# Packed attention and a channel mixer: the first phase's loads in blocks of 128 partitions, and w1 on ScalarE's queue

## The chip, the core and the metric

The kernel runs on one core of one Trainium2 chip: TensorE (PE) for products, VectorE (DVE), ScalarE (ACT) and GpSimd (POOL) for elementwise work, SyncE (SP) to issue transfers, and 16 DMA engines between DRAM and SBUF. SBUF has 128 partitions. Times are device microseconds of one execution. The kernel before took a median of 899.99 us in 3 runs (896.8 to 904.1).

## The reference

Eight batches, eight heads, 576 tokens, 64 numbers per head. 32 packed queries `p` per head attend over all tokens; the 576 queries `q` then attend over the 32 packed results. The heads are joined to 512 columns, and a mixer follows.

```python
def sm_attn(qq, kk, vv):
    s = scale * np.matmul(qq, kk.transpose(0, 1, 3, 2))
    a = np.exp(s - np.max(s, axis=-1, keepdims=True))
    a = a / (np.sum(a, axis=-1, keepdims=True) + 1e-09)
    return np.matmul(a, vv)
p_packed = sm_attn(p, k, v)                 # 8 x 8 x 32 x 64
out = sm_attn(q, p_packed, p_packed)        # 8 x 8 x 576 x 64
# x: 8 x 576 x 512, the heads joined
xt = x.transpose(0, 2, 1)
h = xt @ U @ V                              # over tokens, rank 32
u = x + h.transpose(0, 2, 1)
ch = np.maximum(u @ w_ch1, 0.0) @ w_ch2     # 512 -> 2048 -> 512
return u + ch
```

q, k, v and p are float32. U, V, w_ch1 and w_ch2 come as float64; the kernel reads them as pairs of 32-bit words (`I32`, 8 bytes a number) and makes float32 of them on the chip.

## The kernel before, in words

**Two parts.** The first part works on 16 units, one for each batch and group of four heads (`UN`). A unit loads k (`a_load`, `kx`) and v (`a_load_v`, `vt`), turns k with TensorE (`a_turn`, L205), makes the scores of the packed queries (`a_scores`), their exponentials (`a_softmax`), turns those back (`a_turn_back`), multiplies with v (`a_pack`, L451) and turns the result (`a_heads`). The packed result of each batch goes to DRAM (`ppTd`) and comes back when it is wanted (`ppT`). In the loop of this part (L486) the units are staggered: in iteration i unit i gets its scores, unit i+1 is turned, unit i+2's k and unit i+1's v are asked for. k and v have three buffers each.

Beside the units the first part brings in w1 (`w_ch1`), in 16 pieces of 128 rows by 512 numbers (512 KB of float64 words each): `load_w1` brings the bits, `convert_w1` makes float32 of them with one ScalarE (L75) and four VectorE instructions (L76 to L79). One piece is converted in each iteration (`some_w1`), and the piece two further on is asked for. The bits have two buffers, `bits`, which w2's pieces and the output share later. U and V are loaded in iteration 2 (`load_uv`). From iteration 5 the steps of the attention of batch 0 (`attention(0, res)`, whose first step loads q) run two at a time; in iteration 16 batch 1's q is asked for.

The second part (from L524) goes over 8 batches and 16 blocks of the 2048 hidden columns: `gemm1` (`h_ps`, L84 to L86) and `gemm2` (`o`), each as three float32r products, with the attention of the next batch worked in between as steps, q of the batch after that asked for at block 13, and w2's bits loaded and converted in the first batch. `store` (L604) writes a batch's tokens in four transfers of 256 KB: SBUF gives 128 partitions, DRAM takes two blocks of 64 rows.

**Order.** The first part's instructions are put in order by a scheduler when the program is built, from the order in which they are written and an estimate of their durations; the second part's stand as written. The first products (L84, `h_ps`) therefore stand behind all products of the units on TensorE. Each engine runs its instructions one after another. Every transfer of the program signals one of eight semaphores in turn, and a transfer that takes a semaphore waits until the one that used it before has landed: eight can be in flight, over all queues. All transfers are issued by SP before the change.

**Shapes of the loads before.** k and q (`load_nat`): one transfer for a unit, 128 partitions by 2 by 576 numbers; the partition is (z i), low bit of the head and row block, which in DRAM is a single run of 128 rows. v (`a_load_v`): two transfers of 64 partitions by 4 by 256, and a third for the ninth token of each row block. w1 (`load_w1`): two transfers of 64 partitions by 1024 words.

Of the kernel before, what the change touches and what calls it, by code (L numbers as in the profile page):

```python
# [8 lines left out]
F32 = mybir.dt.float32  # L9
F32R = mybir.dt.float32r  # L10
I32 = mybir.dt.int32
# [8 lines left out]
def packed_attention_mixer_kernel(  # L20
# [26 lines left out]
    nc = tc.nc  # L47
    B, H, S, D = q.shape
# [4 lines left out]
    P = 128  # L53
    SM = 512
    NT = 9
    I = S // NT
    NK = DF // P
    NU = 2 * B
    QW = 512
# [4 lines left out]
    LAST = slice(4 * I, 5 * I)  # L64
# [3 lines left out]
    U, V, w1, w2 = (a.bitcast(I32) for a in (U, V, w1, w2))  # L68
# [24 lines left out]
    def bank():  # L93
        return psT.tile([P, 512], F32, name="t_ps", tag="t")
# [8 lines left out]
    def ppT_tile():  # L103
        return pipe.tile([P, 2, P], F32, name="ppT", bufs=3)
# [21 lines left out]
    def bits_tile():  # L126
        return pipe.tile([P, 512, 2], I32, name="bits", bufs=2)

    chunks = [(x, c) for c in range(NPC) for x in range(4)]
    bits = {}  # L130

    def load_w1(n):
        x, c = chunks[n]
        b = bits["w1", n] = bits_tile()
        for g in range(2):
            r0 = 4 * D * g + D * x
            nc.sync.dma_start(out=b[64 * g:64 * g + 64].rearrange("p x t -> p (x t)"),
                              in_=w1[r0:r0 + D, 2 * QW * c:2 * QW * c + 2 * QW])

    def convert_w1(n):  # L140
        x, c = chunks[n]
        float32_of(conv_tile(I32), conv_tile(F32), bits.pop(("w1", n)), w1t[x][:, QW * c:QW * c + QW])

    def load_w2(kt):
        b = bits["w2", kt] = bits_tile()
        nc.sync.dma_start(out=b.rearrange("p x t -> p (x t)"), in_=w2[kt * P:(kt + 1) * P, :])
# [44 lines left out]


    def load_nat(x, src, b, g):
        nc.sync.dma_start(
            out=x.rearrange("p (h y) -> p h y", h=2),
            in_=src[b, 4 * g:4 * g + 4].rearrange("(h z) (i c) d -> (z i) h (c d)", z=2, c=NT))

    def turn(t, x, h, bank):

        x = x.rearrange("p (h y) -> p h y", h=2)  # L200
        t_ps = bank()
        if h < 2:
            for j in range(4):
                o = P * (2 * (j % 2) + j // 2)
                nc.tensor.transpose(t_ps[:, o:o + P], x[:, h, P * j:P * j + P], ident)  # L205
            nc.scalar.copy(t[:, 2 * h:2 * h + 2, :4 * I].rearrange("p z (j i) -> p j z i", j=4),
                           t_ps.rearrange("p (j z i) -> p j z i", j=4, z=2))
        else:
            for h in range(2):
                nc.tensor.transpose(t_ps[:64, P * h:P * h + P], x[:, h, SM:], ident)  # L210
            nc.scalar.copy(t[:64, :, LAST], t_ps[:64, :2 * P].rearrange("p (h i) -> p h i", h=4))

    def scores(lT, t, g, bank):

# [153 lines left out]
    sA = actx.enter_context(tc.tile_pool(name="sA", bufs=2, reuse_waits="tile"))  # L368
# [4 lines left out]
    pn, pT, pps = {}, {}, {}  # L373
# [4 lines left out]
    def a_load(u):  # L378
        b, g = UN[u]
        ua[u] = {}  # L380
        if g == 0:
            pn[b] = sA.tile([P, 2, 2, D], F32, name="pn")
            for z in range(2):
                nc.sync.dma_start(out=pn[b][:, :, z], in_=p[b].rearrange("(g h) n d -> (h n) g d", g=2))
        ua[u]["x"] = sA.tile([P, 2 * S], F32, name="kx", bufs=3)
        load_nat(ua[u]["x"], k, b, g)

    def a_load_v(u):
        b, g = UN[u]
        vt = ua[u]["v"] = sA.tile([P, 5, 4 * D], F32, name="vt", bufs=3)  # L390
        rows = v[b, 4 * g:4 * g + 4].rearrange("h (i c) d -> i c h d", c=NT)
        main = v[b, 4 * g:4 * g + 4].rearrange("h (i c) d -> i h (c d)", c=NT)[:, :, :8 * D]
        for a in range(2):
            nc.sync.dma_start(out=vt[64 * a:64 * a + 64, :4], in_=main[:, :, 4 * D * a:4 * D * a + 4 * D])
        nc.sync.dma_start(out=vt[:64, 4].rearrange("p (h d) -> p h d", h=4), in_=rows[:, 8])

    def a_p(b):
# [6 lines left out]
    def a_turn(u):  # L404
        b, g = UN[u]
        if g == 0:
            a_p(b)
        ua[u]["t"] = sA.tile([P, 4, 5 * I], F32, name="kT")
        for h in range(3):
            turn(ua[u]["t"], ua[u]["x"], h, bank_a("k"))  # L410

    def a_scores(u):
        b, g = UN[u]
        ua[u]["s"] = scores(pT[b], ua[u]["t"], g, bank_a("s"))

    def a_softmax(u):
        ss = ua[u]["s"]
        mx = sA.tile([P, 3], F32, name="mx")
        sm = ua[u]["sum"] = sA.tile([P, 2], F32, name="sm", bufs=3)
        for r in range(2):  # L420
            nc.vector.tensor_reduce(mx[:, r:r + 1], ss[r], axis=AX.X, op=ALU.max, negate=True)
        nc.vector.tensor_tensor(mx[:, 2:], mx[:, :1], mx[:, 1:2], op=ALU.min)
        e1 = ua[u]["e"] = sA.tile([P, S], F32, name="e1")
        for r in range(2):
            nc.scalar.activation(e1[:, HALF[r]], ss[r], AF.Exp, bias=mx[:, 2:], accum_out=sm[:, r:r + 1])

    def a_turn_back(u):
        e1, sm = ua[u]["e"], ua[u]["sum"]
        eT = ua[u]["eT"] = sA.tile([P, 5, P], F32, name="eT")
        t_ps = bank_a("m")()  # L430
        for kk in range(4):
            turn_back(t_ps, e1, kk, P * kk)
        nc.scalar.copy(eT[:, :4].rearrange("p k x -> p (k x)"), t_ps)
        t_ps = bank_a("m")()
        turn_back(t_ps, e1, 4, 0)
        nc.vector.tensor_copy(eT[:64, 4], t_ps[:64, :P])
        rs = ua[u]["rs"] = sA.tile([P, 1], F32, name="rs")
        nc.vector.scalar_tensor_tensor(rs, sm[:, :1], 1e-9, sm[:, 1:], op0=ALU.add, op1=ALU.add)
        nc.vector.reciprocal(rs, rs)

    def a_pack(u):
        b, g = UN[u]
        eT, vt = ua[u]["eT"], ua[u]["v"]
        p_ps = bank_a("m")()
        vk = vt[:, :4].rearrange("p h x -> p (h x)").rearrange("p (h k d) -> p k h d", h=4, k=4)
        for kk in range(5):
            rows = P if kk < 4 else I
            for h in range(4):
                hs = slice(32 * h, 32 * h + 32)
                rhs = vk[:, kk, h] if kk < 4 else vt[:rows, 4, D * h:D * h + D]  # L450
                nc.tensor.matmul(p_ps[hs, :D], lhsT=eT[:rows, kk, hs], rhs=rhs, start=kk == 0, stop=kk == 4)  # L451
        two = ua[u]["two"] = sA.tile([P, 2, D], F32, name="two")
        nc.scalar.activation(two, p_ps[:, :D].unsqueeze(1).to_broadcast([P, 2, D]), AF.Copy, scale=ua[u]["rs"])
        nc.gpsimd.tensor_copy(ppall[:, b, g], two[:, 0])

    def a_heads(u):
        b, g = UN[u]
        if g == 0:
            pps[b] = ppT_tile() if b == 0 else sA.tile([P, 2, P], F32, name="ppTa")
        z_ps = bank()  # L460
        nc.tensor.transpose(z_ps[:, :P], ua[u]["two"].rearrange("p z d -> p (z d)"), ident)
        nc.scalar.copy(pps[b][:, g], z_ps[:, :P])  # L462
        if g == 1:
            if b == 0:
                ppT[0] = pps[0]
            else:
                nc.sync.dma_start(out=ppTd[b], in_=pps[b].rearrange("p g n -> p (g n)"))

    a_load(0)
    a_load(1)  # L470
    a_load_v(0)
    load_w1(0)
    load_w1(1)
    a_turn(0)
    n_w1 = 0
    first = attention(0, res)

    def some_w1():
        nonlocal n_w1
        if n_w1 < 16:  # L480
            convert_w1(n_w1)
            if n_w1 + 2 < 16:
                load_w1(n_w1 + 2)
            n_w1 += 1

    for i in range(NU + 3):  # L486
        if 0 <= i - 1 < NU:
            a_turn_back(i - 1)
        if i < NU:
            a_scores(i)  # L490
        if i + 1 < NU:
            a_load_v(i + 1)
            a_turn(i + 1)
        if i + 2 < NU:
            a_load(i + 2)
        some_w1()
        if i < NU:
            a_softmax(i)
        if i >= 5:
            for _ in range(2):  # L500
                if first:
                    first.pop(0)()
        if 0 <= i - 2 < NU:
            a_pack(i - 2)
        if 0 <= i - 3 < NU:
            a_heads(i - 3)
        if i == 2:
            uv = load_uv()
        if i == 3:
            prepare_uv(*uv)  # L510
        if i == 13:
            load_w2(0)
            load_w2(1)
        if i == 14:
            fold(0, 0)
        if i == 16:
            steps = attention(1, res)
            steps.pop(0)()
            split_w2(*convert_w2(0))
            load_w2(2)  # L520
# [125 lines left out]
    for b in range(B):  # L646
# [3 lines left out]
        for kt in range(NK):  # L650
# [19 lines left out]
            if kt % 4 == 2 and (b, kt) != (B - 1, NK - 2):  # L670
                n = b * NPC + kt // 4 + 1
# [49 lines left out]
```

## Time and profile before

| | us |
|---|---|
| median of 3 runs | 899.99 |
| lowest, highest | 896.8, 904.1 |
| the profiled execution | 902.82 |
| its span, first to last instruction | 901.0 |
| TensorE busy | 842.1 (93%) |
| VectorE busy | 379.4 (42%) |
| ScalarE busy | 331.5 (37%) |
| GpSimd busy | 93.9 (10%) |

The profile is one execution. Busy time is a share of the whole span and hides that the two parts differ. In rows by stretch, each engine has its busy time and, in brackets, its instructions; PEclk is the clock that TensorE was granted, as a share of full speed; DMA share is the mean busy share of the 16 DMA engines, so that 0.13 is about two of them. In the rows of one tile, three numbers are the shortest, median and longest duration in ns. In the chain of waits, each row is a start, a duration and what ran or was waited for; the rows of SP are the time that it spent issuing.

### The profile page before, as it was taken

What the parts mean: (1) busy time and instruction counts of PE and PEld (TensorE: products, weight loads), DVE (VectorE), ACT (ScalarE), POOL (GpSimd) and SP (SyncE); (2) the same over time, 40 slices, a digit from 0 to 9 for tenths busy, and PEclk for the clock granted to TensorE, in tenths of its full rate; (3) what the DMA queues carried; (4) which work ended last, traced back from release to release, by engine and by line L of the source; (5) the groups of instructions that cost most, each with busy time, mean ns of one, the idle gap of its engine ahead of it and who ended that gap; (6) DMA issues with size and microseconds to landing.
All of it is one profiled execution on the core that took longest, in us unless ns stands there. A gap on an engine that the chain in (4) does not pass through costs nothing.

```text
span 901.0 us, 14507 instructions
## 1 busy us (share of the span) xinstructions
PE 842.1 (93%) x5808; PEld 670.3 (74%) x5808; DVE 379.4 (42%) x892; ACT 331.5 (37%) x952; POOL 93.9 (10%) x111
## 2 busy tenths in 40 slices
PE   5788983999999999999999999999999999999995
PEld 2454653877888887888888888788878887888884
DVE  2455666888534333333334323334343234332320
ACT  3565753544432333333323423234233332332220
POOL 0001122232201010011010101110111001000000
PEclk9787876999999999999999999999999999999998
DMA  9999985223110101001100110010001100000001
GB/s 223 243 255 233 243 202 147 93 95 108 47 45 1 59 11 49 1 1 59 42 6 2 59 59 1 1 59 29 19 1 59 39 21 1 1 17 32 1 3 57
DMA packets 38291, 59.08 MB, mean 66 GB/s; under 512 B 11088, under 2 KB 21200, under 8 KB 38224
## 3 DMA queue, kind: packets, MB, share of 16 engines
q1 hardware_dynamic: 38224, 58.16, 23.8%
q8 instruction: 46, 0.75, 0.4%
q14 instruction: 21, 0.17, 0.1%
HBM read 47.79 MB, written 10.35 MB: 65 GB/s over the span
## 4 chain that ended last, share of the span: by engine, by line
PE 80%; DMA 10%; DVE 5%; ACT 2%; issue 1%; SPq 1%; POOL 0%; DVEq 0%; ACTq 0%
PE o L84 15%; PE o L85 15%; PE o L86 15%; PE h_ps L84 8%; PE h_ps L86 7%; PE h_ps L85 7%; DMA bits<-in_moe_w_ch_dram 5%; PE t_ps L354 3%; DMA kx<-in_k_dram 2%; DMA vt<-in_v_dram 2%; PE t_ps L221 2%; PE t_ps L205 1%; DVE os L76 1%; PE t_ps L296 1%; DVE os L78 1%
## 5 line engine op out<-in xcount | busy, mean ns | idle before, releaser
L84 PE MATMUL o<-w2h,hh 128*128 128x512 f32 x512 | 207.2, 405 | 0.0
L85 PE MATMUL o<-w2l,hh 128*128 128x512 f32 x512 | 202.0, 395 | 0.0
L86 PE MATMUL o<-w2h,hl 128*128 128x512 f32 x512 | 201.8, 394 | 0.0
L580 DVE SCALAR_TENSOR_TENSOR hl<-h_ps,hh 128x256 fp32r<-128x256 f32 x256 | 104.2, 422 | 199.1 <-ACT hj L579 186.7
L84 PE MATMUL h_ps<-ah,wth 128*128 128x320 f32 (+1 forms) x512 | 159.4, 311 | 14.0 <-DVE hl L580 14.0
L577 ACT ACTIVATE hh<-h_ps 128x256 fp32r<-128x256 f32 x256 | 99.0, 388 | 193.0 <-PE h_ps L86 192.5
L85 PE MATMUL h_ps<-al,wth 128*128 128x320 f32 (+1 forms) x512 | 152.8, 298 | 0.0
L86 PE MATMUL h_ps<-ah,wtl 128*128 128x320 f32 (+1 forms) x512 | 152.5, 298 | 0.0
L84 PEld LDWEIGHTS h_ps<-ah,wth 128*128 128x128 f32 x512 | 98.0, 191 | 46.1 <-issue 25.7
L86 PEld LDWEIGHTS o<-w2h,hl 128*128 128x128 f32 x512 | 96.7, 189 | 22.2
L84 PEld LDWEIGHTS o<-w2h,hh 128*128 128x128 f32 x512 | 97.2, 190 | 21.4 <-issue 3.6
L85 PEld LDWEIGHTS o<-w2l,hh 128*128 128x128 f32 x512 | 97.4, 190 | 16.5
L85 PEld LDWEIGHTS h_ps<-al,wth 128*128 128x128 f32 x512 | 98.2, 192 | 1.9
L86 PEld LDWEIGHTS h_ps<-ah,wtl 128*128 128x128 f32 x512 | 98.1, 192 | 0.0
L361 DVE TENSOR_TENSOR wtl<-t_ps,wth 128x256 fp32r<-128x256 f32 x128 | 48.5, 420 | 94.3 <-ACT wth L360 91.0
L360 ACT CAST wth<-t_ps 128x256 fp32r<-128x256 f32 x128 | 43.3, 375 | 109.5 <-PE t_ps L354 98.5
L316 POOL TENSOR_TENSOR al<-aT,ah 128x320 fp32r<-128x320 f32 (+1 forms) x32 | 26.3, 823 | 207.1 <-ACT ah L315 207.0
L260 POOL TENSOR_TENSOR e<-e,m 128x576 f32<-128x576 f32 x16 | 18.7, 1170 | 240.4 <-DVE m L259 240.4
L76 DVE TENSOR_SCALAR os<-os 128x512 f32<-128x512 f32 (+2 forms) x35 | 21.0, 599 | 36.6 <-ACT os L75 36.6
L354 PE MATMUL t_ps<-w1t,ppT 64*32 64x512 f32 x512 | 35.9, 601 | 0.4 <-ACT ppTa L462 0.4
L205 PE MATMUL k_ps<-ident,kx 128*128 128x128 f32 x128 | 24.5, 344 | 11.5 <-DMA kx<-in_k_dram 8.5
L315 ACT CAST ah<-aT 128x320 fp32r<-128x320 f32 (+1 forms) x32 | 13.9, 434 | 53.0 <-DVE aT L314 53.0
(117 smaller groups left out, 1000.1 us busy)
## 6 DMA issues: line engine op xcount, KB each, us to landing
kx<-in_k_dram SPq DMA_DIRECT2D x16, 576.0 KB
x<-in_q_dram SPq DMA_DIRECT2D x16, 576.0 KB
vt<-in_v_dram SPq DMA_DIRECT2D x32, 256.0 KB
bits<-in_moe_w_ch_dram SPq DMA_DIRECT2D x32, 256.0 KB
bits<-in_moe_w_ch_dram SPq DMA_DIRECT2D x16, 512.0 KB
out_dram<-bits SPq DMA_DIRECT2D x32, 256.0 KB
pn<-in_p_dram SPq DMA_DIRECT2D x16, 64.0 KB
vt<-in_v_dram SPq DMA_DIRECT2D x16, 64.0 KB
```

The costliest lines, as they stand in the source:

```text
L76: nc.vector.tensor_single_scalar(t, t, LEAST, op=ALU.max)
L84: nc.tensor.matmul(ps, lhsT=lh, rhs=rh, start=start, stop=False)
L85: nc.tensor.matmul(ps, lhsT=lh, rhs=rl, start=False, stop=False)
L86: nc.tensor.matmul(ps, lhsT=ll, rhs=rh, start=False, stop=stop)
L205: nc.tensor.transpose(t_ps[:, o:o + P], x[:, h, P * j:P * j + P], ident)
L260: nc.gpsimd.tensor_tensor(e, e, m.unsqueeze(2).to_broadcast([P, S // 32, 32]), op=ALU.subtract)
L316: nc.gpsimd.tensor_tensor(al[:, g, ns], aT[:, ns], ah[:, g, ns].bitcast(F32), op=ALU.subtract)
L354: nc.tensor.matmul(f_ps[g][xs], lhsT=ppT[b][gs, g, xs], rhs=w1t[x][gs, QW * c:QW * c + QW], start=True, stop=True)
L360: nc.scalar.copy(hi[:, g], f_ps[g][:, cs])
L361: nc.vector.tensor_tensor(lo[:, g], f_ps[g][:, cs], hi[:, g].bitcast(F32), op=ALU.subtract)
L577: nc.scalar.activation(hh[:, ms], src, AF.Relu)
L580: nc.vector.scalar_tensor_tensor(hl[:, ms], src, 0.0, hh[:, ms].bitcast(F32), op0=ALU.max, op1=ALU.subtract)
```

## The change

All of it concerns the first part's loads and what follows from their new layout.

- w1: a piece is one transfer of 128 partitions instead of two of 64, its DRAM side (x given) being `g d n` with g of 2 and d of 64. It is issued by ScalarE. Even pieces get buffers of their own (`bits2`), so that four pieces can be in flight; four are asked for at the start, and the piece four further on after each conversion. In iterations 3 to 7 two pieces are converted.
- k and q: two transfers for a unit, of 128 partitions by 576 numbers. The partition is now (z i) with z the high bit of the head, so the DRAM side is two blocks of 64 rows. `turn` writes its results to the heads' new places.
- v: four transfers, one for each head, of 128 partitions by 256 numbers; the DRAM side is `a i x`, a of 2 and i of 64. The transfer of the ninth token stays.
- The tile of the packed result on its way to DRAM, `ppTa`, has one buffer instead of two.

```diff
     def load_w1(n):
         x, c = chunks[n]
-        b = bits["w1", n] = bits_tile()
-        for g in range(2):
-            r0 = 4 * D * g + D * x
-            nc.sync.dma_start(out=b[64 * g:64 * g + 64].rearrange("p x t -> p (x t)"),
-                              in_=w1[r0:r0 + D, 2 * QW * c:2 * QW * c + 2 * QW])
+        b = bits["w1", n] = bits_tile() if n % 2 else sA.tile([P, 512, 2], I32, name="bits2")
+        nc.scalar.dma_start(out=b.rearrange("p x t -> p (x t)"),
+                            in_=w1.rearrange("(g x d) n -> x g d n", g=2, x=4)[x, :, :, 2 * QW * c:2 * QW * c + 2 * QW])
...
     def load_nat(x, src, b, g):
-        nc.sync.dma_start(
-            out=x.rearrange("p (h y) -> p h y", h=2),
-            in_=src[b, 4 * g:4 * g + 4].rearrange("(h z) (i c) d -> (z i) h (c d)", z=2, c=NT))
+        heads = src[b, 4 * g:4 * g + 4].rearrange("(z h) (i c) d -> h z i (c d)", z=2, c=NT)
+        for h in range(2):
+            nc.sync.dma_start(out=x[:, S * h:S * h + S], in_=heads[h])
...
     def turn(t, x, h, bank):
...
-            nc.scalar.copy(t[:, 2 * h:2 * h + 2, :4 * I].rearrange("p z (j i) -> p j z i", j=4),
+            nc.scalar.copy(t[:, h::2, :4 * I].rearrange("p z (j i) -> p j z i", j=4),
                            t_ps.rearrange("p (j z i) -> p j z i", j=4, z=2))
...
-            nc.scalar.copy(t[:64, :, LAST], t_ps[:64, :2 * P].rearrange("p (h i) -> p h i", h=4))
+            nc.scalar.copy(t[:64, :, LAST].rearrange("p (z h) i -> p h z i", z=2),
+                           t_ps[:64, :2 * P].rearrange("p (h z i) -> p h z i", h=2, z=2))
...
     def a_load_v(u):
...
-        main = v[b, 4 * g:4 * g + 4].rearrange("h (i c) d -> i h (c d)", c=NT)[:, :, :8 * D]
-        for a in range(2):
-            nc.sync.dma_start(out=vt[64 * a:64 * a + 64, :4], in_=main[:, :, 4 * D * a:4 * D * a + 4 * D])
+        main = v[b, 4 * g:4 * g + 4].rearrange("h (i c) d -> h i (c d)", c=NT)[:, :, :8 * D]
+        for h in range(4):
+            nc.sync.dma_start(out=vt[:, h], in_=main[h].rearrange("i (a x) -> a i x", a=2))
...
     def a_heads(u):
...
-            pps[b] = ppT_tile() if b == 0 else sA.tile([P, 2, P], F32, name="ppTa")
+            pps[b] = ppT_tile() if b == 0 else sA.tile([P, 2, P], F32, name="ppTa", bufs=1)
...
     a_load_v(0)
-    load_w1(0)
-    load_w1(1)
+    for n in range(4):
+        load_w1(n)
...
     def some_w1():
...
             convert_w1(n_w1)
-            if n_w1 + 2 < 16:
-                load_w1(n_w1 + 2)
+            if n_w1 + 4 < 16:
+                load_w1(n_w1 + 4)
...
-        some_w1()
+        for _ in range(2 if 2 < i < 8 else 1):
+            some_w1()
```

The first transfers on SP's queue, before the change (`pn` is p, `kx` is k, `vt` is v, `bits` is w1):

```order
L384 DMA pn<-in_p_dram 128x2x64 x2
L194 DMA kx<-in_k_dram 128x2x576 x2
L394 DMA vt<-in_v_dram 64x4x256 x2
L395 DMA vt<-in_v_dram 64x4x64
L137 DMA bits<-in_moe_w_ch_dram 64x1024 x4
```

The same place after it:

```order
L383 DMA pn<-in_p_dram 128x2x64 x2
L194 DMA kx<-in_k_dram 128x1x576 x4
L393 DMA vt<-in_v_dram 128x1x256 x4
L394 DMA vt<-in_v_dram 64x4x64
L393 DMA vt<-in_v_dram 128x1x256 x4
```

w1 has left SP's queue, k is four transfers of half the size, and the second unit's v follows the first's at once.

The last loads of the first part on SP's queue, before (`x` is q, `ppTd` the packed result's place in DRAM):

```order
L394 DMA vt<-in_v_dram 64x4x256 x2
L395 DMA vt<-in_v_dram 64x4x64
L194 DMA x<-in_q_dram 128x2x576 x2
L467 DMA ppTd_77<-ppTa 128x256
L137 DMA bits<-in_moe_w_ch_dram 64x1024 x4
```

And after (L144 loads bits of w2):

```order
L393 DMA vt<-in_v_dram 128x1x256 x4
L394 DMA vt<-in_v_dram 64x4x64
L194 DMA x<-in_q_dram 128x1x576 x2
L466 DMA ppTd_77<-ppTa 128x256
L393 DMA vt<-in_v_dram 128x1x256 x4
L394 DMA vt<-in_v_dram 64x4x64
L194 DMA x<-in_q_dram 128x1x576 x2
L144 DMA bits<-in_moe_w_ch_dram 128x1024
```

The last v of the first part now stands between the two halves of batch 1's q, and no w1 follows it.

The start of ScalarE's instructions, before (`os` and `bits` are of the conversion, `kT` is turned k, `pT` turned p):

```order
L402 ACT_TABLE_LOAD
L402 ACTIVATE pT<-t_ps 128x256
L206 COPY kT<-k_ps 128x4x2x64 x2
L211 COPY kT<-k_ps 64x4x64
L206 COPY kT<-k_ps 128x4x2x64
L75 ACTIVATE os<-bits 128x512 x2
```

And after:

```order
L401 ACTIVATE pT<-t_ps 128x256
L75 ACTIVATE os<-bits_111 128x512
L75 ACTIVATE os<-bits 128x512
L204 COPY kT<-k_ps 128x4x2x64
L75 ACTIVATE os<-bits_115 128x512
L135 DMA bits_187<-in_moe_w_ch_dram 128x1x1024
L204 COPY kT<-k_ps 128x4x2x64
L75 ACTIVATE os<-bits 128x512
L209 COPY kT<-k_ps 64x2x2x64
L135 DMA bits<-in_moe_w_ch_dram 128x1x1024
```

Four issues of w1 come ahead of these rows; the fifth and sixth stand among the copies of the first k, and the conversions of the first pieces stand ahead of or between these copies.

## The prediction, made before the changed kernel was run

> **What bounds the kernel now.** I read the slices of the page first, then the stretches, then the chain of waits, then the transfers.
>
> ```profile
> span 901.0 us, 14507 instructions
> DMA  9999985223110101001100110010001100000001
> GB/s 223 243 255 233 243 202 147 93 95 108 47 45 1 59 11 49 1 1 59 42 6 2 59 59 1 1 59 29 19 1 59 39 21 1 1 17 32 1 3 57
> ```
>
> A slice is 22.5 us. For five or six of them all 16 DMA engines are busy; afterwards they are nearly idle. The first phase (k, v and w1 come in, the packed keys are made) therefore depends on transfers, the rest on TensorE. The stretches show it by engine; the last three lie in the second part of the run.
>
> ```profile
> core 0: us, PE busy (x) PEld busy (x) DVE busy (x) ACT busy (x) POOL busy (x), PEclk, DMA share, GB/s
> 0.00:25.00 25.00, 14.36 (x76) 8.39 (x76) 6.65 (x20) 9.81 (x23) 0.85 (x7) 1.00 0.99 231
> 25.00:50.00 25.00, 19.32 (x215) 10.90 (x214) 12.86 (x42) 12.34 (x35) 0.48 (x2) 0.66 0.97 236
> 50.00:75.00 25.00, 21.18 (x328) 13.07 (x325) 13.19 (x38) 16.98 (x45) 2.11 (x5) 1.00 1.08 250
> 75.00:100.00 25.00, 22.94 (x238) 13.38 (x238) 12.47 (x33) 14.23 (x39) 4.94 (x7) 0.59 0.99 235
> 100.00:125.00 25.00, 22.72 (x324) 13.29 (x323) 17.94 (x53) 18.72 (x55) 1.72 (x6) 1.00 1.09 247
> 222.00:226.00 4.00, 4.00 (x21) 3.43 (x21) 2.87 (x5) 1.35 (x3) 1.31 (x1) 1.00 0.79 241
> 245.00:267.00 22.00, 22.00 (x159) 18.31 (x158) 7.70 (x22) 8.07 (x25) 1.16 (x1) 1.00 0.13 48
> 431.00:453.00 22.00, 22.00 (x159) 18.30 (x158) 7.83 (x21) 8.12 (x26) 1.16 (x1) 1.00 0.13 48
> ```
>
> To 125 us the engines are full at 231 to 250 GB/s. In 222 to 226 us a pair of q loads has them to itself (share 0.79, that is 12.6 of 16). In 245 to 267 us only stores of `out` run: share 0.13, 2.1 engines of 16, at 48 GB/s. That row decides this prediction.
>
> The chain shows how the first phase ends, and the timeline of TensorE what comes last there; the third fence is the group of the first products (L84).
>
> ```profile
> 137.01 4.77 DMA bits<-in_moe_w_ch_dram
> ...
> 145.01 3.53 DMA bits<-in_moe_w_ch_dram
> 148.62 0.67 ACT os L75
> ...
> 152.05 0.64 PE h_ps L84
> ```
> ```profile
> 127.38 2.83 PE L451 MATMUL m_ps<-vt,eT 128*32 128x64 f32 x80
> ...
> 133.34 0.61 PE L84 MATMUL h_ps<-ah,wth 128*128 128x320 f32 x1
> ```
> ```profile
> L84 PE MATMUL h_ps<-ah,wth x512: 280/302/636, 133.3 to 871.5; 128*128 128x256 f32 x86, 128*128 128x320 f32 x85
> ```
>
> The last v is used at 127.4 us, the first product starts at 133.3, six microseconds later, and after twelve matmuls TensorE stalls until 152.05 for the last pieces of w1. Without that stall the product of 133.3 could have started at 149 at no loss (152.05 less the 3 us of twelve matmuls). I count from **149 us**: whatever the first phase takes beyond it is added to the time.
>
> **The stores, the nearest relative of the new loads.** The first row is the store's instructions, the next two are SP's timeline, the last two are the transfers of 244 to 268 us in 40 slices.
>
> ```profile
> L604 SPq DMA_DIRECT2D out_dram<-bits x32: 511/2030/4857, 244.3 to 881.0; - x32
> ```
> ```profile
> 244.29 5.02 SPq L604 DMA_DIRECT2D out_dram<-bits  x3
> ```
> ```profile
> 245.70 8.44 SPq L604 DMA_DIRECT2D out_dram<-bits  x2
> ```
> ```profile
> GB/s 0 0 20 14 41 24 58 41 48 55 48 55 48 55 48 55 48 55 48 55 48 55 48 55 48 55 48 55 48 55 48 55 48 55 48 55 75 55 41 0
> DMA packets 522, 1.08 MB, mean 45 GB/s; under 512 B 8, under 2 KB 8, under 8 KB 520
> ```
>
> All four stores of a batch have been issued by 254 us, and still only two engines work until 267. So it is not one transfer after another: all four share the same pair. What they have in common is the shape. SBUF gives 128 partitions, and the DRAM side (`[c0:c0+5:4]`, L605) is two blocks of 64 rows. The q load of 222 us, whose DRAM side is a single run of 128 rows, had 12.6 engines. Every load that the change rewrites gets the store's shape turned round: the outer dimension in DRAM is 2 (`(z h)` for k and q, `a` for v, `g` for w1) and SBUF has 128 partitions. Before, k and q were `(h z)` with z and i merging into one run of 128 rows, and v and w1 went in halves of 64 rows. So I expect two engines for each, the same two on both queues, at 48 GB/s in all.
>
> The Trainium skill ("DMA: Bandwidth & Descriptors", section "Why a DMA increments its semaphore by 16 and not by 1") says that a transfer takes the largest number of engines up to 16 that divides the slowest dimension of both sides; with 2 and 128 that is two, the lowest-numbered ones, and the stores agree (0.13 of 16). By that page's 27 GiB/s per engine, 58 GB/s for two, the sum below would come out at an estimated 1270 us; the stores measured 48.
>
> **The sum, part by part.** Sizes are from the transfers of the page.
>
> ```profile
> kx<-in_k_dram SPq DMA_DIRECT2D x16, 576.0 KB
> x<-in_q_dram SPq DMA_DIRECT2D x16, 576.0 KB
> vt<-in_v_dram SPq DMA_DIRECT2D x32, 256.0 KB
> bits<-in_moe_w_ch_dram SPq DMA_DIRECT2D x32, 256.0 KB
> ...
> pn<-in_p_dram SPq DMA_DIRECT2D x16, 64.0 KB
> vt<-in_v_dram SPq DMA_DIRECT2D x16, 64.0 KB
> ```
>
> What the two engines must bring before the first product can start: k, 16 x 576 KB = 9.44 MB; v's main part, 32 x 256 KB = 8.39 MB; w1, 8.39 MB; q of the first attention, 2 x 576 KB = 1.18 MB; and the first half of the next q, 0.59 MB, which stands ahead of the last v in SP's order. That is 27.99 MB, and at 48 GB/s **583 us**. The rest of the phase (p, v's ninth token, U, V, three blocks of w2, the packed keys to DRAM) keeps its shape, about 5 MB; at the phase's 240 GB/s (next fence) some **20 us**, since its share on these two engines queues with the others. First landing 1 us, last v to first product 7 us. The first product is then at 1 + 583 + 20 + 7 = 611 us, 462 after 149.
>
> Will the two engines ever be idle? A unit (k, v, one w1 piece: 590 + 524 + 524 KB) takes 34 us on them; its arithmetic took some 8 us before (125 us for 16 units), and k and v each have three buffers, so SP is up to two units ahead. The weak places are SP's waits on TensorE for a buffer and, near the end, on the first attention for q's tile, with the last v behind it. I add **5 us**, and up to 40 in the range.
>
> The other edits are free under this cover. **Issues**: SP issues about 30 transfers more over the run; the dearest usual issue is 0.6 us (fence below) against 2.7 to 6.1 us that such a transfer holds the two engines. **w1 on ScalarE's queue**: SP no longer waits there for a free buffer, but the issue now blocks ScalarE. The third and fourth store above held SP for up to 4.86 us each because the two engines took no more; sixteen w1 issues will hold ScalarE likewise, longer when both queues are full, and kT, eT and the exponentials stand behind it. It costs nothing while the two engines work anyway; if that cover went, 16 x 4.86 = 78 us. **Two conversions** in five iterations move DVE work forward and add none. The new **turn** copies as many elements per instruction. **ppTa with one buffer** makes ScalarE wait for a 128 KB store issued two units earlier, 68 us by then, behind at most eight transfers of 6 us. In the second part, **q** of a batch takes 1.18 MB / 48 = 25 us instead of 4; its first half (12 us) is wanted three steps after the issue, and a step is (871.5 - 133.3) / 128 = 5.8 us: covered, and TensorE's 760 us there stay. The stall at 137 to 152 us goes, because w1 is converted by the eleventh unit; the late thing is then the last v.
>
> ```profile
> L394 SPq DMA_DIRECT2D vt<-in_v_dram x32: 595/616/1452, 2.8 to 117.0; - x32
> ```
> ```profile
> GB/s 55 325 236 233 224 279 215 268 244 272 134 176 344 249 268 212 243 218 327 292 214 254 220 221 140 304 235 256 256 216 245 277 204 293 218 229 229 236 326 220
> DMA packets 26351, 31.22 MB, mean 240 GB/s; under 512 B 10237, under 2 KB 19326, under 8 KB 26337
> ```
>
> (The last fence is the transfers of 0 to 130 us.) The profiled execution took 902.8 us with a span of 901.0; 902.8 + 462 + 5 = **1370 us**. The median of the runs is 900.0, three microseconds lower, which matters to nothing here.
>
> **Bounds.** No row has a load on two engines. The best slices of the store ran at 55 GB/s: 509 us instead of 583, total 1291. The best slice of the first phase, 344 GB/s on 16 engines, is 21.5 each or 43 for two: 651 us, total 1433, and 1473 with 40 us of idle engines. I take 48, the row of the nearest shape. Range 1290 to 1475.
>
> **Rivals.** *Faster: the engines follow the side that is written.* In the stores the written side is the one with the outer 2; in the new loads it is SBUF with 128 partitions, and every other load here has equal outer dimensions on both sides, so no row separates this from "both sides". If it holds, all 16 engines write to all partitions. Then the halves that crowd 64 partitions are gone, and 31.22 MB at the best slice's 344 GB/s would take 91 us instead of 130. TensorE alone is busy for 100.5 us of the first 125, so the first product would start at about 115 rather than 149: 869 us. It decides as soon as a new load shows a share over 0.5. The Trainium skill, same page, section "Rules for kernel authors", speaks for this case where it says that two transfers to disjoint partition halves should be one of 128 partitions. I give it 9%: the same section warns that an outermost dimension under 16 confines a transfer to so many engines.
>
> *No change:* 16 engines, but TensorE with its granted clock of 0.59 to 0.66 in two stretches and ScalarE's issues use up the gain: 895 to 905 us, 3%.
>
> *Slower by little: each transfer gets another pair.* With up to eight in flight, some four pairs would give 8 x 23 = 184 GB/s, 152 us for the 28 MB, first product near 180 us, 934 us. The four stores speak against it, which would then have shown four times 0.13. 3%.
>
> **The numbers.** Two fixed engines: 85%; the range holds about 79 of these 85 points, and the other 6 are more idle time than 40 us, or a rate outside the bounds. 1% is about what a measurement of this kernel can tell from no change. Faster 0.09, same 0.03, slower 0.88 (85 and 3).
>
> **What would show it.** Right: the slices show a DMA share of 1 to 2 tenths at about 50 GB/s for some 17 of the 40 slices; the chain becomes DMA of kx, vt and bits for over 40% of the span; TensorE's clock rises in the first phase as it waits; the first product lies near 610 us; ScalarE's queue shows w1 issues of several microseconds. Wrong: a DMA share over 0.5 in the first 100 us. That would mean that the split goes by the written side, and the whole sum falls.

## The result, and the profile after

The changed kernel takes **1355.8 us** (median of 4 runs, 1354.6 to 1356.2) where the kernel before takes 900.0 (4 runs, 896.8 to 904.1): a ratio of 1.506, 95% interval 1.500 to 1.512. The forecast was 1370, range 1290 to 1475. The profiled execution took 1354.6 us with a span of 1352.7, which is 451.7 more than before.

The page of the changed kernel: its span, slices (33.8 us each now), queues (q1 is SP's, q10 is ScalarE's) and chain (SPq and ACTq are the time that SP and ScalarE spend issuing):

```profile
span 1352.7 us, 14539 instructions
PE   0101133212102434439999999999999999999996
PEclk9999995555555555659999999999999999999999
DMA  1111121111111211213310010010100100100001
GB/s 50 51 51 55 51 71 54 52 50 56 51 55 57 69 55 55 83 61 94 95 55 16 27 52 1 30 41 1 53 26 3 55 15 28 51 1 1 32 1 40
q1 hardware_dynamic: 34896, 49.76, 10.8%
q10 hardware_dynamic: 2080, 8.39, 1.5%
PE 52%; SPq 30%; DMA 11%; DVE 3%; ACT 1%; issue 1%; POOL 0%; DVEq 0%; ACTq 0%
```

In the first 17 slices the DMA share is one tenth, three times two, with 50 to 57 GB/s in most. w1's 8.39 MB have a queue of their own (q10) and yet the two queues together move little more than the 48 GB/s that the stores' one did. The same by stretches:

```profile
core 0: us, PE busy (x) PEld busy (x) DVE busy (x) ACT busy (x) POOL busy (x), PEclk, DMA share, GB/s
0.00:50.00 50.00, 3.32 (x12) 2.06 (x12) 2.91 (x6) 3.62 (x6) 0.85 (x7) 1.00 0.13 50
100.00:200.00 100.00, 19.14 (x178) 11.27 (x178) 7.36 (x27) 10.44 (x29) 0.24 (x1) 1.00 0.17 59
300.00:400.00 100.00, 21.91 (x222) 10.99 (x222) 20.42 (x54) 15.12 (x42) 3.46 (x6) 0.52 0.15 54
500.00:600.00 100.00, 37.88 (x348) 22.00 (x348) 12.25 (x35) 15.70 (x44) 7.08 (x17) 0.57 0.21 69
620.00:640.00 20.00, 20.00 (x133) 17.03 (x132) 17.53 (x29) 10.68 (x27) 7.87 (x6) 1.00 0.33 96
```

In the first 50 us, when nothing but the new loads and a few small ones run, the share is 0.13: the very figure of the stores before. By the packet records of this trace two packets are in flight between 6 and 20 us, over both queues together, apart from moments of overlap where one follows another: the two queues share one pair of engines. Until the first product at least two packets are in flight in all but 0.4 us of 590.8, so nothing shows the pair idle. TensorE is busy for 3 us of the first 50. The end of the phase, in the first products' group, the chain, and the timelines of ScalarE and TensorE:

```profile
L84 PE MATMUL h_ps<-ah,wth x512: 278/294/616, 590.8 to 1323.2; 128*128 128x256 f32 x86, 128*128 128x320 f32 x85
```
```profile
577.18 2.65 SPq L393
...
583.12 0.69 SPq L194
...
583.85 2.78 SPq L194
...
586.73 4.37 SPq L144
...
591.19 11.21 DMA ppTd<-ppTa
...
602.50 0.28 ACT ppTa L461
...
602.82 1.97 PE t_ps L203 x8
604.79 0.27 PE h_ps L84
```
```profile
602.50 0.43 ACT L461 COPY ppTa<-t_ps 128x128 f32<-128x128 f32 x2 [11.90 <-DMA ppTd<-ppTa]
```
```profile
604.44 0.62 PE L84 MATMUL h_ps<-ah,wth 128*128 128x320 f32 x1
```

The last v is issued by 580 us, the first product starts at 590.8, and then TensorE stands again, from 593 to 603: ScalarE waits to write the last packed result into the one buffer of `ppTa`, where the result before it still waits for its store, behind the second half of q and a block of w2. The products go on at 604.4, where before they went on at 152.05. The difference, 452.4, is within a microsecond the 451.7 us of the spans: the whole loss lies before this point.

### The profile page after: what moved, and what is told of

The parts are those of the page before. It is cut to its first block, busy times and chain, and to the rows that moved or that the text cites. A ratio compares the mean times of both kernels' runs of the same rounds, so it can differ in the third digit from the quotient of the medians.

```text
span 1352.7 us, 14539 instructions
## 1 busy us (share of the span) xinstructions
PE 873.9 (65%) x5808; PEld 683.6 (51%) x5808; DVE 377.0 (28%) x892; ACT 331.5 (25%) x952; POOL 91.4 (7%) x111
## 3 DMA queue, kind: packets, MB, share of 16 engines
q10 hardware_dynamic: 2080, 8.39, 1.5%
## 4 chain that ended last, share of the span: by engine, by line
PE 52%; SPq 30%; DMA 11%; DVE 3%; ACT 1%; issue 1%; POOL 0%; DVEq 0%; ACTq 0%
SPq L393 20%; PE o L84 10%; PE o L85 10%; PE o L86 10%; PE h_ps L84 5%; PE h_ps L85 5%; PE h_ps L86 5%; DMA kx<-in_k_dram 5%; SPq L194 4%; SPq L394 4%; PE t_ps L353 2%; DMA bits<-in_moe_w_ch_dram 2%; DMA vt<-in_v_dram 2%; DMA x<-in_q_dram 2%; SPq L383 1%
## 5 line engine op out<-in xcount | busy, mean ns | idle before, releaser
L84 PE MATMUL o<-w2h,hh 128*128 128x512 f32 x512 | 207.0, 404 | 0.0
L203 PE MATMUL k_ps<-ident,kx 128*128 128x128 f32 x128 | 34.1, 424 | 260.5 <-DMA kx<-in_k_dram 233.8
L203 PEld LDWEIGHTS k_ps<-ident,kx 128*128 128x128 f32 x128 | 23.2, 216 | 274.6 <-issue 141.2
L84 PE MATMUL h_ps<-ah,wth 128*128 128x320 f32 (+1 forms) x512 | 158.8, 310 | 0.3 <-DVE hl L580 0.2
L84 PEld LDWEIGHTS h_ps<-ah,wth 128*128 128x128 f32 x512 | 97.8, 191 | 32.1 <-issue 26.2
L84 PEld LDWEIGHTS o<-w2h,hh 128*128 128x128 f32 x512 | 97.1, 190 | 21.7 <-issue 3.9
L204 ACT COPY kT<-k_ps 128x512 f32<-128x512 f32 x32 | 18.6, 585 | 205.6 <-PE k_ps L203 142.5
L227 PE MATMUL m_ps<-ident,e 128*128 128x128 f32 x64 | 19.8, 412 | 63.6 <-ACT e L424 63.6
L227 PEld LDWEIGHTS m_ps<-ident,e 128*128 128x128 f32 x64 | 11.5, 205 | 77.7 <-ACT e L424 68.8
```

The costliest lines, as they stand in the source:

```text
L84: nc.tensor.matmul(ps, lhsT=lh, rhs=rh, start=start, stop=False)
L227: nc.tensor.transpose(t_ps[:, o:o + P], src[:, c0:c0 + P], ident)
```

## The experiments

### No DRAM side of two blocks

The first run mends the shapes and keeps the rest: each load to 128 partitions, w1 on ScalarE's queue, four pieces in flight, as many transfers. The turn of k (left out of the cut) and the fold follow the new layout. The fold multiplies the rows of w1 that belong to a head with the batch's packed result; eight such products give a block of the weights of the first products.

```diff
 # k, q
-        heads = src[...].rearrange("(z h) (i c) d -> h z i (c d)", z=2, c=NT)
+        heads = src[...].rearrange("(h z) (i c) d -> h (z i) (c d)", z=2, c=NT)
 # v: row block outermost; k's columns are turned in that order too
-            nc.sync.dma_start(out=vt[:, h], in_=main[h].rearrange("i (a x) -> a i x", a=2))
+            nc.sync.dma_start(out=vt[:, h], in_=main[h].rearrange("i (a x) -> i a x", a=2))
 # w1: a pair of neighbouring heads instead of heads x and 4 + x
-                            in_=w1.rearrange("(g x d) n -> x g d n", g=2, x=4)[x, :, :, ...]
+                            in_=w1[P * x:P * x + P, ...]
 # fold
-                gs = slice(64 * g, 64 * g + 64)
-                nc.tensor.matmul(f_ps[g][xs], lhsT=ppT[b][gs, g, xs], rhs=w1t[x][gs, QW * c:QW * c + QW],
+                gs = slice(64 * (x % 2), 64 * (x % 2) + 64)
+                nc.tensor.matmul(f_ps[g][xs], lhsT=ppT[b][gs, g, xs], rhs=w1t[2 * g + x // 2][gs, QW * c:QW * c + QW],
```

> The changed kernel with every load still going to 128 partitions, the same number of transfers, w1 still on ScalarE's queue, but with no DRAM side of two blocks: k and q in two transfers whose 128 rows are one run, w1 as 128 neighbouring rows (a pair of heads; the fold takes the halves accordingly), v with the row block outermost (64 by 2) and k's columns turned in the same order. Theory (two blocks in DRAM confine a transfer to two engines): all 16 engines again, DMA share over 0.5 in the first 100 us, time 865 to 890. Rival (the cost is ScalarE held by its issues, the larger number of transfers, or 128 partitions as such): all of these remain, so still over 1200.

Measured: **902.9 us**, ratio to before 1.002 (1.000 to 1.005). The loss of 456 us is gone, and the rival that kept the queue, the number of transfers and the 128 partitions is refuted. The page's slices of this run:

```profile
DMA  9898843330101010010001010011001100000001
GB/s 315 250 316 247 270 145 95 95 124 32 45 1 45 18 55 1 1 59 27 21 1 59 27 33 1 13 48 47 1 15 46 58 1 1 1 23 25 1 3 58
```

All engines are back, at 247 to 316 GB/s in the first five slices. But the time is not the 865 to 890 expected; where the gain went is taken up below.

### Sixteen blocks, and four

Only w1 is altered, in the changed kernel: 128 rows by 1024 words, read in the order of f blocks (f=16 here, f=4 in the second run). The fold is left as it is and so gets its rows in another order.

```diff
-                            in_=w1.rearrange("(g x d) n -> x g d n", g=2, x=4)[x, :, :, 2 * QW * c:2 * QW * c + 2 * QW])
+                            in_=w1[P * x:P * x + P, 2 * QW * c:2 * QW * c + 2 * QW].rearrange("(e f) n -> f e n", f=16))
```

> The changed kernel, but a piece of w1 is 128 neighbouring rows read in the order of 16 blocks of 8 (stride 16 rows), so the DRAM side's outer dimension is 16 instead of 2; size, partitions, queue and number of transfers are as in the change, k, v and q keep two blocks. The rows land in another order than the fold wants, so the result is another one; the work is the same. Theory (engines = outer count): w1's 8.39 MB leave the pair but for an eighth, 7.34 MB / 48 GB/s = 153 us less, about 1203 (1185 to 1230). Rival (any DRAM side that is not one run is held to two engines, or the written side or the queue decides): 1356 as before.

> As the run with 16 blocks, but w1's DRAM side is 4 blocks of 32 rows (result again in another row order). Theory (engines = outer count, the lowest-numbered ones): half of w1 stays on the pair, 4.19 MB / 48 GB/s = 87 us less than the change, about 1268 (1250 to 1290). Rival (two blocks are a special case, anything above spreads over 16): about 1203. Rival (anything but one run gets two): 1356.

Measured: 16 blocks **1230.7**, 4 blocks **1285.0**, against 1355.8 with 2 (one run each; the changed kernel's own runs lie within 2 us). Their first products, the run with 16 first:

```profile
L84 PE MATMUL h_ps<-ah,wth x512: 280/302/615, 466.6 to 1199.4; 128*128 128x256 f32 x86, 128*128 128x320 f32 x85
```
```profile
L84 PE MATMUL h_ps<-ah,wth x512: 280/302/616, 520.6 to 1253.6; 128*128 128x256 f32 x86, 128*128 128x320 f32 x85
```

With size, partitions, queue and number of transfers equal, the outer count orders the times. The rivals do not fit: two blocks are not a special case (4 lies between), and a DRAM side in pieces is not always held to two engines (16 is far better). The traces show the count of engines directly. These are the transfers of the first 30 us in 40 slices, with 16 blocks and with 4, each with the page's row of w1's queue:

```profile
DMA  0058969999999983111111111111111114897111
GB/s 0 0 121 213 213 158 282 269 253 235 246 225 206 260 220 92 57 51 50 49 52 49 52 49 49 49 52 49 52 49 49 49 52 87 270 232 170 31 51 51
```
```profile
q10 hardware_dynamic: 2304, 8.39, 2.7%
```
```profile
DMA  0035222222222222222222222222222221111111
GB/s 0 0 72 75 82 93 68 87 93 87 106 95 103 103 100 100 106 95 100 106 100 106 100 103 103 106 100 106 100 106 106 111 84 60 49 51 51 57 51 51
```
```profile
q10 hardware_dynamic: 2112, 8.39, 1.9%
```

While w1's first pieces move, 16 blocks bring the share to 0.8 and more in most slices; 4 blocks hold it at 0.2 and some at about 100 GB/s, twice the 51 of two engines. Between 6 and 20 us of the run with 4 blocks, k's two-block packets are on their way beside w1's, and yet about four packets are in flight in all: k's pair is among w1's four. The packet counts say the same. Sixteen pieces of 128 rows are 2048 packets of 4096 bytes; the queue counted 2304, 2112 and, with two blocks, 2080. The rest are packets of 4 bytes: 16, 4 and 2 for each piece, the outer count each time.

The sizes are off. 125 us were saved instead of 153 (1230.7 lies just above its range), and 71 instead of 87, about 0.8 of each. The ratio of the two savings, 0.57, is the one that the theory wants (4.19 / 7.34 = 0.57). The pair was not left waiting: until the first product at least two packets were in flight in all but 0.5 us with 16 blocks and 1.7 us with 4. But a packet took longer when more engines worked. w1's packets took 256 and 187 ns on average against 164 in the changed kernel, so that, at an estimate, the eighth of w1 left on the pair took 33 us instead of the 22 of the sum. k's and q's packets took 99 ns instead of 96.

### k and q alone

```diff
 # kernel before, with the changed kernel's turn
-        nc.sync.dma_start(out=x.rearrange("p (h y) -> p h y", h=2),
-            in_=src[...].rearrange("(h z) (i c) d -> (z i) h (c d)", z=2, c=NT))
+        heads = src[...].rearrange("(z h) (i c) d -> h z i (c d)", z=2, c=NT)
+        for h in range(2):
+            nc.sync.dma_start(out=x[:, S * h:S * h + S], in_=heads[h])
```

> The kernel before with one part of the change: k and q in two transfers of two blocks each, and the turn that goes with it; v and w1 as before, all on SP's queue. Theory: the pair must bring k and the first q, 10.62 MB, and an eighth of the other 19.4 MB, in all 13 MB / 48 GB/s = 271 us, first product near 279 us, time about 1035 (1000 to 1090). Rival (the loss comes from v's small transfers or from w1 on ScalarE's queue): within 20 us of 900.

Measured: **1100.3 us** (one run), ten beyond the range. k and q are the largest part by bytes and alone cost 200 us, without any w1 on ScalarE's queue and without the four transfers of v; the rival is out. The first product started at 340.8 us rather than 279. In the stretch of 0 to 340 us the profile of this run shows a mixed state, a share of 0.39 that is six engines on average:

```profile
0.00:340.00 340.00, 146.50 (x1260) 79.57 (x1260) 79.92 (x214) 79.97 (x208) 15.70 (x31) 0.61 0.39 100
```

At least two packets were in flight in all but 3.3 us of the 340.8. Of the 62 us missing, 25 are batch 1's q (1.18 MB / 48 GB/s), which I had left out of the sum. For the rest the packets' time is enough: k's and q's packets of 2304 bytes took 113 ns on average, beside loads on all engines, against 96 in the changed kernel. Over 5037 packets on two engines that is an estimated 41 us.

### ScalarE's queue

```diff
 # changed kernel
-        nc.scalar.dma_start(out=b.rearrange("p x t -> p (x t)"),
+        nc.sync.dma_start(out=b.rearrange("p x t -> p (x t)"),
```

> The changed kernel once more, unaltered, beside the next two on one chip: 1355 (1350 to 1360).

> The changed kernel with w1 issued by SP instead of ScalarE, the shape of two blocks kept. Theory (the two engines bound the phase, whoever issues): 1340 to 1375, for the same 28 MB pass the same pair. Rival (ScalarE held in its issues leaves the pair idle): 1300 or less. Rival (SP, held by w1's buffers, brings k and v late): 1390 or more.

Measured beside each other on one chip: 1355.9 for the changed kernel, **1356.7** with w1 on SP's queue. Who issues makes no difference that these runs show. The same exchange in the mended kernel, with the fold's products in another order (below):

> The mended kernel with the fold in the new order, and w1's pieces issued by SP instead of ScalarE. Theory (with 16 engines an issue takes half a microsecond and the queue does not matter): within 6 us of the run with w1 on ScalarE's queue. Rival (SP stands waiting for a free buffer of w1 with k and v behind it): 10 to 25 us slower than that run.

897.1 against 894.8, within the 6 us expected; the intervals of the ratio to before touch (0.994 to 0.999, 0.990 to 0.995).

### The single buffer

```diff
 # changed kernel
-            pps[b] = ppT_tile() if b == 0 else sA.tile([P, 2, P], F32, name="ppTa", bufs=1)
+            pps[b] = ppT_tile() if b in (0, B - 1) else sA.tile([P, 2, P], F32, name="ppTa", bufs=1)
```

> The changed kernel, with the last batch's packed result in a free buffer of ppT instead of the single ppTa. In the profile of the change ScalarE waits from 590.6 to 502.5+100 (602.5) us for the store of the batch before, which queues behind the second half of batch 1's q on the two engines, and TensorE stands from 593 to 603. Theory (that stall is added to the time): 8 to 11 us less, about 1346. Rival (w2's blocks or q, queued on the same two engines, are late next): the same 1355.

Measured: **1347.8**, 8.1 less than the changed kernel on the same chip (4 runs each, within 2.1 us). Most of the stall of 11 us was added to the time. The prediction had costed this edit at nothing.

### The other edits alone

Here k, q, v and w1 have the shapes of the kernel before, and w1's halves come through ScalarE's queue with four pieces in flight and two conversions in five iterations; `ppTa` has one buffer.

```diff
 # changed kernel, with load_nat, turn and a_load_v of the kernel before, and
+        for g in range(2):
+            r0 = 4 * D * g + D * x
+            nc.scalar.dma_start(out=b[64 * g:64 * g + 64].rearrange("p x t -> p (x t)"),
+                                in_=w1[r0:r0 + D, 2 * QW * c:2 * QW * c + 2 * QW])
```

> The change without its new load shapes: k and q in one transfer of 128 rows, v and w1 in halves of 64 rows as before; w1 on ScalarE's queue, four pieces in flight, two converted in five iterations, ppTa with one buffer remain. Theory (the loss is the shape alone, and converting w1 early removes the stall for its last pieces, 137 to 152 us of the kernel before): 880 to 897. Rival (ScalarE's blocked issues or the single ppTa cost time at any shape): 905 to 940.

Measured: **908.8**, ratio 1.008 (1.004 to 1.012). So the other edits do not cause the loss of 456 us. But they gain nothing where I had expected 880 to 897, and the time lies in the rival's range of 905 to 940: the edits cost some 9 us at the shapes of before. Which of them costs it is not shown, for the runs spread from 899.1 to 912.4 and the profiled execution is one of the fastest, 899.7. In it the first 150 us read:

```profile
0.00:150.00 150.00, 101.83 (x1280) 61.18 (x1281) 77.14 (x216) 77.93 (x215) 19.73 (x40) 0.88 0.98 232
```

w1's pieces no longer stall the end, but the engines are full throughout (0.98) at 232 GB/s, and the first product starts at 146.5 us against the 149 I count for before. The stall of 137 to 152 us was the end of a phase that transfers bound; w1 brought earlier takes its share from k and v.

### Where the mended kernel's gain went

The mended kernel's first product started at 126.7 us, 22 before the 149, and the time was that of before:

```profile
L84 PE MATMUL h_ps<-ah,wth x512: 280/292/415, 126.7 to 871.6; 128*128 128x256 f32 x86, 128*128 128x320 f32 x85
```

From the first product to the last of L84 it took 744.9 us, where the kernel before took 722 without its stall. The fold is why. The groups of the fold's products, in the kernel before and in the mended one, busy time behind the bar:

```profile
L354 PE MATMUL t_ps<-w1t,ppT 64*32 64x512 f32 x512 | 35.9, 601 | 0.4 <-ACT ppTa L462 0.4
```
```profile
L360 PE MATMUL t_ps<-w1t,ppT 64*32 64x512 f32 x512 | 62.1, 595 | 0.0
```

Each product takes as long, but fewer run at once. A product uses half of the partitions (64 rows of w1) and 32 of the array's columns. With heads x and 4 + x in a tile the eight products of a fold use eight places (half, columns). With neighbouring heads they use four, each twice. I first put it down to the order. In the second order neighbours alternate between the halves, in the third also between the two banks of accumulators that they write:

```diff
+        for g in range(2):                      # third order: for y in range(2)
+            for x in range(4):                  #                  g = (x + y) % 2
+                xs = slice(32 * x, 32 * x + 32)
+                gs = slice(64 * (x % 2), 64 * (x % 2) + 64)
```

> The mended kernel (every load to 128 partitions, none with two blocks in DRAM) with the fold's products in another order. In the first mended kernel both products of one w1 tile lie in the same half of the partitions, so neighbours no longer overlap: the fold's products took 62.1 us in all instead of 35.9 before. Here neighbours alternate between the halves again. Theory (the mended loads gain what the crowded phase cost, and the fold had eaten it): 26 us less than the first mended run, about 876 (866 to 886). Rival (the first phase is bound by TensorE and ScalarE anyway, and nothing is gained by freeing the DMA engines): 895 to 905.

> The mended kernel with the fold's products in a third order: neighbours alternate both between the halves of the partitions and between the two banks they write. In the second order they alternated between the halves, with four in a row to one bank, and still took 61.5 us in all. Theory (products overlap when half and bank both change, as in the kernel before): 35.9 us for the fold, 26 us less than the second order, 869 (862 to 876). Rival (they overlap only when both use the same 32 columns of the array, as before): 890 to 897, the fold unchanged at 61.5 us.

Measured: **894.8** (ratio 0.993, 0.990 to 0.995) and **902.8** (1.002, 0.999 to 1.005), with 61.5 and 61.6 us for the fold: the order is not it, and both runs miss what I expected (866 to 886 and 862 to 876). The last run gives each product its place. Three tiles of w1 stay runs of 128 rows, the fourth comes in two halves:

```diff
+        heads = ((0, 1), (2, 3), (5, 6), (7, 4))[x]
...
+                half = (x + g) % 2
+                y = x // 2 if g == 0 else (3, 2, 2, 3)[x]
```

> The mended kernel with the fold's eight products each in a place of its own: the tiles of w1 hold the heads (0, 1), (2, 3), (5, 6) and (7, 4), so that a group of 32 columns meets each half of the partitions once, as in the kernel before; the last tile comes in two transfers of 64 rows. In the three mended folds so far only four places (half, 32 columns) were used, each twice, and 16 matmul records took 1.92 us instead of 1.09. Theory (two products in one place follow each other, whatever the order and the bank): the fold 35.9 us in all, 22 to 28 us less than 901, about 876 (866 to 884). Rival (something else in the second part holds it, so that the freed first phase is worth nothing): 893 to 903.

Measured: **886.8 us**, ratio 0.984 (0.981 to 0.987): the best of all, though short of the 866 to 884 expected. Its first products, its fold, and sixteen recorded matmuls in a row, two for each of a fold's eight products, in the timelines of before, of the first mended kernel, of the second and third order, and of this one:

```profile
L84 PE MATMUL h_ps<-ah,wth x512: 280/292/417, 132.4 to 853.8; 128*128 128x256 f32 x86, 128*128 128x320 f32 x85
```
```profile
L365 PE MATMUL t_ps<-w1t,ppT 64*32 64x512 f32 x512 | 36.4, 601 | 0.0
```
```profile
163.66 1.09 PE L354 MATMUL t_ps<-w1t,ppT 64*32 64x512 f32 x16
```
```profile
163.71 1.94 PE L360 MATMUL t_ps<-w1t,ppT 64*32 64x512 f32 x16
```
```profile
163.06 1.92 PE L360 MATMUL t_ps<-w1t,ppT 64*32 64x512 f32 x16
```
```profile
165.21 1.92 PE L361 MATMUL t_ps<-w1t,ppT 64*32 64x512 f32 x16
```
```profile
168.84 1.09 PE L365 MATMUL t_ps<-w1t,ppT 64*32 64x512 f32 x16
```

This run brings back two things at once, eight places and neighbours in the same 32 columns, so it alone does not refute the third order's rival. The starts of the sixteen records do. In the kernel before and in this run eight start within 47 ns, and the other eight from 453 ns on. In the second and the third order four start within 21 ns, and the next fours at 453, 882 and 1311 ns after the first. The first four products of these orders lie in four different groups of columns, so products of different columns do overlap. What fits all five folds is that products in one place follow each other.

The fold got back 25.7 us of TensorE, and the profiled execution became 17.9 us shorter (901.1 to 883.2), the median 16.2. The time from the first product to the last of L84 is 721.4 us again, 23.5 less than in the first mended kernel; but the first product starts at 132.4 us, almost 6 later than with w1 all in runs of 128 rows. Why the second order was 8 us faster than the first and the third with the same fold is not settled.

## Why the prediction was right

**The step that carried it** was to read the stores as the relative of the loads: share 0.13 of 16 for a transfer whose DRAM side is two blocks, four of them in flight on the same pair. The changed kernel's first 50 us show 0.13 and 50 GB/s for loads. That the written side might decide (9%) is refuted: here the side that is read has the 2. The runs with 4 and 16 blocks carry it from "two blocks are slow" to "the outer count in DRAM sets the number of engines". This is the rule that the Trainium skill states ("DMA: Bandwidth & Descriptors", section "Why a DMA increments its semaphore by 16 and not by 1"), and the traces agree for the DRAM side (shares, packet counts, and the ratio of the savings). Whether a small outer count on the SBUF side would do the same is not shown: no run varies it. By the 27 GiB/s per engine of the same page of the Trainium skill (section "Specifications") the time would have been an estimated 1270; the measured 1355.8 decides for the stores' 48 GB/s.

**The sum.** Forecast: 611 us for the first product, 5 of idle engines, 467 over before. Measured: 590.8, then a stall to 603, 451.7 over before. So the 20 us for the small loads and the 5 for idle engines were too much. 27.99 MB by about 587 us (the last v is in use shortly before the first product) are 47.7 GB/s: the rate was right, and the small loads hid beside it. The sum was 25 us too high there and 11 us too low by the stall that it lacked. That the total missed by only 15 us is in part luck.

**The term that failed: ppTa at nothing.** I took 68 us between two stores and at most eight transfers of 6 us ahead of each, and called it covered. ScalarE waited for it five times:

```profile
ACT ppTa L461 <- DMA ppTd<-ppTa: 57.4, 5, 15.5
```

Four of these lie under the transfers; the last, 11.9 us, has no cover, because nothing of the first phase is left to wait for. The run with another buffer gave back 8.1. That store of 128 KB took 11.2 us, behind the second half of q and a block of w2.

**The covers that held.** SP's issues and ScalarE's cost nothing, though they held their engines much longer than before:

```profile
L194 SPq DMA_DIRECT2D kx<-in_k_dram x32: 543/2507/15748, 1.7 to 537.9; - x32
L393 SPq DMA_DIRECT2D vt<-in_v_dram x64: 543/3554/18637, 36.1 to 577.2; - x64
```
```profile
0.73 29.02 ACTq L135 DMA_DIRECT2D bits<-in_moe_w_ch_dram  x4
```

I had foreseen the hold for ScalarE, from the store's 4.86 us, and used 0.6 us for SP, where v's median is 3.55 and the longest 18.6. ScalarE was held for 29 us by its first four issues and could not convert or copy anything; two later ones took 16.3 together, the other ten 0.5 each. In the chain the phase therefore appears as SPq (30%) more than as DMA (11%), where I had said DMA for over 40%. With w1 on SP's queue the time was the same (1356.7), so ScalarE's hold lay beside the pair's work. q's longer load in the second part was covered as said: from the first product to the last L84 of `h_ps` it took 732 us after the change (1323.2 - 590.8, a stall of 11 us included) and 738 before (871.5 - 133.3, with its 16 us of stall): 721 and 722 without.

**The forecast of the clock was wrong**: I said that TensorE's clock would rise in the first phase; it was granted 0.50 to 0.57 in the stretches from 200 to 600 us, where it waited most of the time.

**The rival on the other side** was worth less than its price. With all engines and 128 partitions the first product came at 126.7 us, not 115, and the best whole kernel reached 886.8, not 869.

## What to carry to other kernels

Read the outermost dimension of both sides of every transfer before judging how it is spread: 128 partitions in SBUF are worth nothing if DRAM gives them in two blocks, and a store of the same kernel may already show the price (here 48 GB/s instead of 240). When a load's layout is mended, follow it to the products that use it: neighbouring heads in a tile made the loads faster and put two products in one place of the array, which took the gain back: eight places instead of four returned most of it. An engine that waits for its own earlier store needs cover up to the last store, not on average.

## What the runs showed of the hardware that I had not expected

- TensorE had a lower granted clock when it had less to do: 0.52 in 300 to 400 us of the changed kernel with 21.9% busy, 1.00 in the second part with 100%. In the first 200 us the profile says 1.00, but the transposes of k took 431 ns on average in 0 to 100 us and 426 in 200 to 300, where it says 0.50, so the figure of the first 200 us is probably not the clock of that time.
- A full pair of DMA engines holds the issuing engine: ScalarE for 29 us over four issues, SP for up to 18.6 us in one. In the kernel before, the longest issue of v took 1.5 us.
- The time of a packet grew with the engines at work: w1's 4096 bytes took 164 ns on average with two blocks, 187 with 4 and 256 with 16.
- Eight small products in eight places of the array take 1.09 us for sixteen records, in four places 1.92 to 1.94, whatever the order and the bank.
